# Six more groups of the first layer by seven products, one mixed weight array in place of raw weights, and first products copied from bank to bank, in a new order

## The chip, the cores and the metric

The kernel runs on one core of a Trainium2 chip. The metric is the device time of one execution in microseconds (us). Engines are called as in the profile: PE is TensorE (PEld its weight loads), DVE VectorE, ACT ScalarE, POOL GpSimd, SP SyncE, which issues most stores and the transposing transfers.

## The reference

Attention over four batches with eight heads, 768 positions and head dimension 64, each position seeing 96 local positions and 8 global ones, with a bias by distance; its output, with the heads side by side, is a matrix x of 3072 tokens by 512, which goes through a feed-forward layer with a squared relu.

```python
    scores = scale * np.matmul(q, k.transpose(0, 1, 3, 2))
    ...
    is_global = pos[None, :] < int(n_global)
    is_local = (rel >= 0) & (rel < int(n_local))
    ...
    scores = scores + bias[None, :, :, :]
    scores = np.where(keep, scores, -1000000000.0)
    ...
    return np.matmul(a, v).astype(np.float32)
...
    h = np.maximum(x @ w_in, 0.0)
    return (h * h @ w_out).astype(np.float32)
```

Here w_in is 512 by 2048 and w_out 2048 by 512.

## The kernel before

**Tiles and stages.** The 3072 tokens are worked on in eight halves of 384 (half 0 to half 7, two to a batch). For each half the scores of the local and global positions are made (PE sp, L715), put through exp on ScalarE (ex), weighed with a mask on VectorE (phat), multiplied with v (PE av, L776), divided (rec, tm), and transposed by a DMA from SP's queue into xt, the transposed x. q, k and v come in by DMAs from POOL's queue (sq, sk, v) and are transposed by SP (q<-sq, k<-sk). kb and vb hold the parts of k and v that a half needs of its neighbour.

**Layer 1.** The hidden 2048 are 16 blocks of 128. *Plain* (function layer1, L822): a block and 384 tokens are four matmuls 384 columns wide into a bank hps of PSUM; a relu (L847 on ACT, L849 on DVE) brings it to hr in SBUF, and a square of two blocks (L861, L863) to h2 (named h in the profile). *By seven products* (layer1_group): two blocks of the near half of the hidden (block 0 to 7) and the two that lie eight further (the far half) are taken as one 2 by 2 scheme with the two halves of the 512 inner and the two halves of the 384 tokens. Seven products p1 to p7 of four matmuls 192 columns wide (L925) take the place of the 16 plain ones. For them there are mixed weights (sums and differences of quarters of w_in, in_mix, made once, L886) and mixed tokens (x_mix, made for each half, L903). The products p1, p6, p7 and p4 add up in one bank, "a", p5 and p3 in a second, "f", p2 in a third, "c". In between, sums are copied to SBUF (kept, L353 on ACT, L355 on DVE) and added back by a custom add with relu on DVE (L983), or a plain relu takes the result (L989 on ACT, L991 on DVE); squares follow (L1005, L1007). In half 2 another way is used (SEEDS 1): the kept p1 is copied back into bank "f" and p2 adds onto it.

Halves 0 and 1, which open the program, are all plain (in part 256 and 128 columns wide). Half 2 has two such groups, halves 3 to 7 have three each, 17 in all; the rest of their blocks is plain.

**Layer 2** works on pairs of 128-token tiles by seven products as well (layer2_pair, L1145, with token sums mixed, L1110, and adds into y, L1207) or plain (layer2, L1059), and stores y to the output.

**The order.** Jobs of PE are listed as a program, and a table, ORDER, fixes the order of the work on all engines: words for PE's jobs (p, with a bank behind the point), DVE (d), ACT (a), SP (s), POOL's loads (l, with a job to wait for behind @) and g. Two tables of letters, LETTERS and LAYER1, set for each half the sequence in which the products of the groups and the plain blocks (s) are listed. Each engine runs its instructions strictly in its row.

## Time and profile before

| | |
|---|---|
| time, median of three runs | 202.02 us (201.25 to 203.07) |
| time of the profiled execution | 201.98 us |
| its span | 200.2 us |
| PE busy | 191.8 us (96%), clock 1.00 |
| DVE busy | 177.7 us (89%) |
| ACT busy | 146.3 us (73%) |
| POOL busy | 66.6 us (33%) |

In a group's row of the profile stand the line, engine, operation, what is written and read, the count, then busy time and the mean ns of one, then the idle time of the engine just ahead of them with what ended it. The chain of waits is read in order of time: start, length, what. Matmuls are pipelined, so that the duration of one holds part of the next; the distance between two starts is what one adds. L numbers in the profile are those of the kernel before; in the new one the same lines stand 6 to 43 further down (L353 is L359, L355 L361, L822 L833, L886 L901, L903 L921, L925 L943, L983 L1001, L989 L1007, L1007 L1025, L1110 L1139, L1145 L1175).

### The profile page before, as it was taken

Reading aid. Unit: us, or ns where it says so; the run is one execution under the profiler, and the core shown is the slowest. Engines: PE = TensorE matmul, PEld = TensorE weight load, DVE = VectorE, ACT = ScalarE, POOL = GpSimd, SP = SyncE. Lnnn points to the kernel's source line nnn. Section 1 sums busy time; section 2 is a strip of 40 time slices with the busy share of each in tenths; the row PEclk is TensorE's granted clock in tenths of the full one; section 3 lists DMA queues with packets and bytes.
Section 4 is the critical chain, followed back from the end, with each engine's and each line's share of the span. In section 5 each row is a group of like instructions: output and inputs, shape, how many; then the busy total and the mean of one; then the engine's idle time right before and its main releaser. Section 6 shows DMA issues by size and latency. Waiting matters only on the chain.

```text
span 200.2 us, 5881 instructions
## 1 busy us (share of the span) xinstructions
PE 191.8 (96%) x2349; PEld 160.8 (80%) x2349; DVE 177.7 (89%) x448; ACT 146.3 (73%) x310; POOL 66.6 (33%) x82
## 2 busy tenths in 40 slices
PE   7797999999999999999999998999999999999993
PEld 3575899856888687789877897889879899889992
DVE  6889778999995989999999997999999899899780
ACT  6899857998836679988888758987986866365311
POOL 5998537537102910970108700670000000000000
PEclk9999999999999999999999999999999999999999
DMA  5999999999998999999999995699734420020214
GB/s 161 177 149 181 198 181 171 207 194 155 149 224 89 143 123 243 134 149 105 272 119 93 152 140 114 146 150 155 199 75 142 105 75 2 0 108 0 108 52 157
DMA packets 106987, 27.52 MB, mean 137 GB/s; under 512 B 97104, under 2 KB 104016, under 8 KB 106960
## 3 DMA queue, kind: packets, MB, share of 16 engines
q0 software_dynamic: 74944, 13.11, 87.4%
q1 hardware_dynamic: 30816, 13.45, 32.1%
q10 hardware_dynamic: 1200, 0.59, 1.1%
q8 instruction: 18, 0.29, 0.7%
q14 instruction: 9, 0.07, 0.2%
HBM read 27.26 MB, written 6.29 MB: 168 GB/s over the span
## 4 chain that ended last, share of the span: by engine, by line
PE 76%; DMA 13%; POOL 6%; DVE 3%; issue 1%; SPq 0%; ACT 0%; POOLq 0%; DVEq 0%
PE yps L1145 29%; PE hps L822 17%; PE hps L925 17%; DMA w_in_sb<-in_moe_w_in_dram 5%; PE sp L715 4%; PE av L776 4%; PE yps L1059 4%; DMA q<-sq 3%; DMA xt<-tm 3%; DMA v<-in_v_dram 3%; POOL w_mix L491 2%; POOL v L491 2%; DVE hr L983 1%; PE trp L650 1%; POOL sk L491 1%
## 5 line engine op out<-in xcount | busy, mean ns | idle before, releaser
L822 PE MATMUL hps<-xt,w_in_sb 128*128 128x384 f16 (+2 forms) x336 | 45.3, 281 | 0.8 <-DMA w_in_sb<-in_moe_w_in_dram 0.8
L728 ACT ACTIVATE ex<-sp 128x512 f16<-128x512 f32 x66 | 35.3, 619 | 4.4 <-PE sp L715 3.6
L1145 PEld LDWEIGHTS <-h 128*128 128x128 f16 x376 | 34.1, 98 | 4.7
L822 PEld LDWEIGHTS <-w_in_sb 128*128 128x128 f16 x336 | 28.0, 98 | 8.7 <-DMA w_in_sb<-in_moe_w_in_dram 1.2
L1145 PEld LDWEIGHTS <-mixed 128*128 128x128 f16 x272 | 25.1, 98 | 3.1 <-DVE mixed L1110 0.2
L847 ACT ACTIVATE hr<-hps 128x384 f16<-128x384 f32 (+1 forms) x43 | 21.7, 548 | 7.6 <-PE hps L822 7.6
L983 DVE CUSTOM_DVE_ANT_0 hr<-hps,kept 128x384 f16<-128x384 f32 x49 | 25.8, 549 | 1.1 <-PE hps L925 0.7
L491 POOL DMA_DIRECT2D sq<-in_q_dram x19 | 17.0, 900 | 27.2 <-DMA xt<-tm 13.2
L353 ACT COPY kept<-hps 128x384 f32<-128x384 f32 x43 | 20.3, 491 | 7.9 <-PE hps L925 5.8
L353 ACT COPY y<-yps 128x256 f32<-128x256 f32 (+2 forms) x36 | 12.7, 381 | 18.0 <-PE yps L1145 16.5
L491 POOL DMA_DIRECT2D v<-in_v_dram x24 | 21.6, 918 | 12.1 <-DMA k<-sk 9.6
L491 POOL DMA_DIRECT2D sk<-in_k_dram x19 | 17.1, 902 | 25.2 <-DMA xt<-tm 9.4
L925 PEld LDWEIGHTS <-in_mix 128*128 128x128 f16 x272 | 23.0, 98 | 2.4 <-DVE x_mix L903 0.5
L925 PE MATMUL hps<-x_mix,in_mix 128*128 128x192 f16 x204 | 23.7, 247 | 0.2 <-DVE x_mix L903 0.2
L1145 PE MATMUL yps<-w_mix,h 128*128 128x256 f16 (+1 forms) x192 | 22.7, 264 | 0.0
L1145 PE MATMUL yps<-w_out_sb,h 128*128 128x256 f16 (+1 forms) x184 | 22.5, 268 | 0.0
L1145 PE MATMUL yps<-w_mix,mixed 128*128 128x256 f16 (+1 forms) x184 | 22.3, 268 | 0.0
L752 DVE TENSOR_TENSOR phat<-ex,mask 128x1024 f16<-128x1024 f16 (+1 forms) x36 | 21.0, 594 | 0.1
L1005 ACT ACTIVATE h<-hr 128x768 f16<-128x768 f16 x22 | 18.5, 848 | 1.2 <-DVE hr L983 0.7
L925 PEld LDWEIGHTS <-w_in_sb 128*128 128x128 f16 x204 | 17.4, 98 | 1.5
L861 ACT ACTIVATE h<-hr 128x768 f16<-128x768 f16 (+1 forms) x23 | 17.0, 768 | 1.7 <-DVE hr L849 0.9
L925 PE MATMUL hps<-xt,w_in_sb 128*128 128x192 f16 x136 | 15.8, 246 | 0.0
(110 smaller groups left out, 347.9 us busy)
## 6 DMA issues: line engine op xcount, KB each, us to landing
out_dram<-y SPq DMA_DIRECT2D x23, 256.0 KB, 2.6
v<-in_v_dram POOLq DMA_DIRECT2D x24, 128.0 KB, 6.4
sk<-in_k_dram POOLq DMA_DIRECT2D x19, 128.0 KB, 6.0
sq<-in_q_dram POOLq DMA_DIRECT2D x19, 128.0 KB, 5.0
w_in_sb<-in_moe_w_in_dram POOLq DMA_DIRECT2D x4, 512.0 KB, 10.2
w_out_sb<-in_moe_w_out_dram POOLq DMA_DIRECT2D x4, 512.0 KB, 10.5
y<-in_k_dram ACTq DMA_DIRECT2D x2, 256.0 KB, 4.8
y<-in_q_dram SPq DMA_DIRECT2D x2, 256.0 KB, 4.2
```

The source lines that it names most:

```text
L353: nc.scalar.copy(out=out, in_=in_)
L491: dma = nc.gpsimd.dma_start(out=dst, in_=src[x.b, :, r0 + t * P:r0 + (t + 1) * P, :] .rearrange("h p d -> p h d"))
L715: nc.tensor.matmul(sp[h][:, i, :], lhsT=lhsT, rhs=x.q[rows, r % HT, a, :], start=True, stop=True)
L728: nc.scalar.activation(out=st["ex"][:, h], in_=sp[h], func=AF.Exp, scale=scale)
L752: eng(e).tensor_tensor(out=x.phat[a][:, :, t0:t0 + n], op=ALU.mult, in0=st["ex"][:, :, i0:i0 + 2 * n].rearrange("p e (t b) c -> p e t (b c ...
L822: nc.tensor.matmul(st["ps"][:, i * n:(i + 1) * n], lhsT=w_in_sb[:, kk, m * P:(m + 1) * P], rhs=x.xt[:, kk, c0:c1], start=kk == 0, stop=kk ...
L847: nc.scalar.activation(out=o, in_=i, func=AF.Relu)
L861: nc.scalar.activation(out=h2, in_=hr, func=AF.Square)
L925: nc.tensor.matmul(st[name][:, i * HC:(i + 1) * HC], lhsT=left(i, kk), rhs=right(kk), start=fresh and i == kk == 0, stop=kk == KK - 1, ski ...
L983: nc.vector._custom_dve(TENSOR_ADD_SAT, out=hidden(which)[:, :, cols], in0=sums(name), in1=st[kept], s0=LARGEST, s1=0.0)
L1005: nc.scalar.activation(out=h2, in_=hr, func=AF.Square)
L1145: nc.tensor.matmul(st[bank_name][:, 0:n], lhsT=a(m), rhs=b(m)[:, cols], start=fresh and m == 0, stop=m == HK - 1, skip_group_check=not fresh)
```

## The change

Half 2 works three groups by seven products where it worked two, and halves 3 to 7 four where they worked three: 23 groups for 17. The fourth group is made of blocks 0, 1, 8 and 9 (GROUPS gets a 0), so the mixed weights are wider: 8 blocks instead of 6, 2048 elements a partition each instead of 1536. To save room, the third mixed weight is written over a quarter of the raw w_in, in two pieces, once the plain matmuls of the far half that read it are done (far_jobs); the others are three arrays in place of four.

In halves 3 to 7 (SEEDS 2, "copied"; 20 groups) p1's sum isn't kept in SBUF for p2's add; it is copied from bank "a" to a new bank "c" (across), p2 adds onto it there, and its result goes through a plain relu. p6, which reuses bank "a", also waits for that copy. For layer 2 the same form is written down but not used. Groups of matmuls in one bank now set the start flag with the bank's first matmul alone.

The table ORDER is new from end to end.

```diff
-SEEDS = [0, 0, 1, 0, 0, 0, 0, 0]
+SEEDS = [0, 0, 1, 2, 2, 2, 2, 2]
...
-GROUPS = [1, 2, 3]
-LETTERS = {3: "abcdefg", 2: "ABCDEFG", 1: "1234567"}
-LAYER1 = {2: "sasbcsdABCsesDEsFGfsgs", 3: "as123456b7cdsAeBCfgDsEFsG",
-          4: "AasBbCscDEdefF123ss45gG67", 5: "1A2BCDs3E45sF6abcdefgGs7s",
-          6: "AsabcdBeCDfsEss1F234567Gg", 7: "AsaBbcdCDseEfF1234s567Gsg"}
+GROUPS = [0, 1, 2, 3]
+LETTERS = {0: "HIJKLMN", 3: "abcdefg", 2: "ABCDEFG", 1: "1234567"}
+LAYER1 = {h: "abAcBdCeDfEgFG12H3I4J5K6L7MN" if h in [3, 5, 7, 6, 4] else "abAcBdCeDfEgFG12s3s4s5s67" for h in range(2, 8)}
...
-ORDER = """d1 s8 g2 a4 p0.0 a6 s10 d12 a0 d13 l1 d3 l4 l2 l3 d146 a26 d15 d20 a22 l0 a30 d9 d21 a18 d5 a17
...
+ORDER = """d146 g2 d1 d12 d13 d3 l1 s8 l4 a4 a6 a0 a17 d5 d22 d15 p0.0 d7 a26 a9 l3 a16 a20 l2 l5 l10 l6 l0
...
+    def copied(self, job, costs, emit, needs=()):
+
+        op = self.after(job, costs, emit, needs)
+        op.takes, op.users = 1, [[op]]
+        return op
...
+        if ms[-1] >= NFT // 2:
+            far_jobs.append((ms, job))
...
-                    mix = const.tile([P, 4, KK, near.stop - near.start], FP16, name="in_mix")
-                    in_mix.extend(mix[:, i] for i in range(4))
+                    mix = const.tile([P, 3, KK, near.stop - near.start], FP16, name="in_mix")
+                    in_mix.extend([mix[:, 0], mix[:, 1], w[1][0], mix[:, 2]])
...
+            wide = near.stop - near.start
+            for cols in [slice(0, wide)] if i != 2 else [slice(2 * P, wide), slice(0, 2 * P)]:
+                in_mix_ops[i].append(plan.add(
+                    {"DVE": 0.1 + KK * (cols.stop - cols.start) * 0.00053},
+                    lambda e, f=weight_sum, cols=cols: f(e, cols=cols),
+                    needs + w_in_op + (in_mix_ops[0] if i == 2 else []), plan.rank + MIX[4]))
...
-        seeded = SEEDS[x.hb]
+        seeded, copied = SEEDS[x.hb] == 1, SEEDS[x.hb] == 2
...
         def p1():
-            keep(run("a", True, weight(0, 0), plain(0, 0)), "a", "keep1")
+            job = run("a", True, weight(0, 0), plain(0, 0))
+            if not copied:
+                keep(job, "a", "keep1")
+                return
+
+            def across(e):
+                st["c"] = bank([P, 512], FP32, "hps")
+                copy(e, sums("c"), sums("a"))
+            ops["keep1"] = plan.copied(job, {"ACT": 0.41, "DVE": 0.48}, across)
+            st["users", "c"] = ops["keep1"].users
 
         def p2():
-            if seeded:
+            if copied:
+                give(run("c", False, weight(1, 0), plain(1, 0), [ops["keep1"]]), "c", 0, 0)
+            elif seeded:
                 give(run("f", False, weight(1, 0), plain(1, 0), [ops["seed"]]), "f", 0, 0)
             else:
                 give(run("c", True, weight(1, 0), plain(1, 0)), "c", 0, 0, "keep1")
...
+    for own, op in zip((slice(NFT // 2 + 2, NFT), slice(NFT // 2, NFT // 2 + 2)), in_mix_ops[2]):
+        op.needs.extend(job for ms, job in far_jobs
+                        if any(own.start <= m < own.stop for m in ms))
```

The new table moves rows on every engine. Two places show how; numbers behind names tell tiles apart.

ScalarE where half 3's first layer begins, beside half 2's second layer (y) and later scores (ex): before, the first product of a group (hps_1884) is kept in SBUF.

```order
L728 ACTIVATE ex_1879<-sp_1856 128x512
L728 ACTIVATE ex_1879<-sp_1857 128x512
L728 ACTIVATE ex_1899<-sp_1843 128x512
L353 COPY y_1824<-yps_1755 128x256
L353 COPY kept_1903<-hps_1884 128x384
L728 ACTIVATE ex_1815<-sp_1792 128x512
L728 ACTIVATE ex_1899<-sp_1844 128x512
L353 COPY kept_1939<-hps_1884 128x384
```

And after, where the first product (hps_1873) goes to a second bank (hps_1888):

```order
L359 COPY y_1869<-yps_1851 128x256
L735 ACTIVATE ex_1871<-sp_1790 128x512
L359 COPY hps_1888<-hps_1873 128x384
L359 COPY kept_1890<-hps_1861 128x384
L359 COPY y_1824<-yps_1813 128x256
L735 ACTIVATE ex_1871<-sp_1791 128x512
L1007 ACTIVATE hr_1921<-hps_1888 128x2x192
L359 COPY kept_1936<-hps_1873 128x384
```

The copy across stands where a keep stood, and the relu of p2 (hr_1921 from hps_1888) has come to ScalarE.

VectorE at the end of half 2's first layer, before: hr are relus or adds with relu, h2_1436 the squares that layer 2 reads, mixed_1804 the first of its token sums.

```order
L1007 TENSOR_TENSOR h2_1436<-hr_1677 128x768
L991 TENSOR_SCALAR hr_1691<-hps_1574 128x2x192
L1007 TENSOR_TENSOR h2_1436<-hr_1683 128x768
L355 COPY kb_885<-k_884 128x4x96
L355 COPY kb_885<-k_884 128x4x32
L863 TENSOR_TENSOR h2_1436<-hr_1732 128x768
L863 TENSOR_TENSOR h2_1436<-hr_1753 128x768
L1110 TENSOR_TENSOR mixed_1804<-h2_1436 128x1024
```

After, the same place:

```order
L1001 ISA hr_1763<-hps_1684,kept_1720 128x2x192
L1009 TENSOR_SCALAR hr_1741<-hps_1675 128x2x192
L1025 TENSOR_TENSOR h2_1469<-hr_1704 128x768
L1025 TENSOR_TENSOR h2_1469<-hr_1741 128x768
L1025 TENSOR_TENSOR h2_1469<-hr_1711 128x768
L878 TENSOR_TENSOR h2_1469<-hr_1722 128x768
L921 TENSOR_TENSOR x_mix_1831<-xt_1550 128x384
L1139 TENSOR_TENSOR mixed_1833<-h2_1469 128x1024
```

The four squares of the half's end stand in one row behind the relu hr_1741, with a part of the next half's x_mix between them and the token sum.

More of the change, by code (lines that the diff above doesn't have):

```diff
@@ L1126, in layer2_pair @@
         y_bufs = Buffer("y", 4), Buffer("y", 4)
[L1127 removed]
+        seeded = PAIR_SEEDS[len(seeds)] == 1 and not final
+        copied = PAIR_SEEDS[len(seeds)] == 2 and not final
         seeds.append(seeded)
@@ L1238, in p1, with across @@
             x.h2_buf.used_by(job)
-            keep(job, "a", "keep1")
+            if not copied:
+                keep(job, "a", "keep1")
+                return
+            def across(e):
+                st["c"] = bank([P, 512], FP32, "yps")
+                copy(e, st["c"][:, 0:HN], st["a"][:, 0:HN])
+            ops["keep1"] = plan.copied(job, {"ACT": 0.31, "DVE": 0.36}, across)
+            st["users", "c"] = ops["keep1"].users
         def p2():
-            if seeded:
+            if copied:
+                job = run("c", False, plain(x, i, 1), weight(1, 0), [ops["keep1"]])
+            elif seeded:
                 job = run("f", False, plain(x, i, 1), weight(1, 0), [ops["seed"]])
```

164 lines of the change are left out of this document (84 added, 80 removed).

## The prediction

> **What bounds the kernel now.** I read the page first, then the stretches of the span, the waits of TensorE and the chain that ended last. All times are of the profiled execution; 201.98 us of its time are 200.2 us of span and 1.78 us around it, and it lies 0.04 us under the median of 202.02 of the runs, so a change of the span is taken as the same change of the time.
>
> The page, its first lines of busy time and its chain of work by engine:
>
> ```profile
> span 200.2 us, 5881 instructions
> PE 191.8 (96%) x2349; PEld 160.8 (80%) x2349; DVE 177.7 (89%) x448; ACT 146.3 (73%) x310; POOL 66.6 (33%) x82
> PE 76%; DMA 13%; POOL 6%; DVE 3%; issue 1%; SPq 0%; ACT 0%; POOLq 0%; DVEq 0%
> ```
>
> TensorE is busy 96% of the span and is three quarters of the chain. The view by stretches (columns: stretch and its length, then busy us of PE, weight loads, DVE, ACT, POOL, granted clock, DMA share, GB/s) says where the other 4% lie:
>
> ```profile
> 23.60:196.80 173.20, 172.28 (x2054) 146.66 (x2054) 158.29 (x387) 126.23 (x266) 47.75 (x55) 1.00 1.16 133
> 100.00:110.00 10.00, 9.84 (x120) 7.68 (x115) 9.83 (x25) 8.73 (x21) 4.29 (x5) 1.00 1.13 108
> 110.00:120.00 10.00, 9.85 (x139) 9.21 (x137) 9.79 (x26) 6.56 (x15) 3.63 (x5) 1.00 1.92 146
> 120.00:130.00 10.00, 9.43 (x117) 7.84 (x115) 8.62 (x22) 8.98 (x19) 3.21 (x4) 1.00 0.69 130
> ```
>
> From 23.6 us to the last matmul TensorE lacks 0.92 us of 173.20, and 0.88 of these lie between 100 and 130 us. The clock is 1.00 throughout. VectorE has 158.29 of 173.20: 14.9 us of air, the next engine to run out. What comes ahead of 23.6 us is a load, in the chain (start, length, what):
>
> ```profile
> 14.16 9.41 DMA w_in_sb<-in_moe_w_in_dram
> 23.62 1.92 PE hps L822 x16
> ```
>
> So the span is: an opening set by a queue of loads, 173 us of nearly gapless matmuls, and a tail. The tail, by the timeline's last rows:
>
> ```profile
> 196.82 0.37 ACT L353 COPY y<-yps 128x256 f32<-128x256 f32 x1 [1.05 <-PE yps L1145]
> 197.22 0.33 SPq L1230 DMA_DIRECT2D out_dram<-y  x1
> ```
>
> The last matmul ends at 196.8, a copy, a store, and the span's end at 200.2: 3.4 us.
>
> **The change, part by part.** *Fewer, narrower products.* A group by seven products has 28 matmuls of 192 columns in place of 16 of 384. Six groups more make 96 of the wide ones go and 168 narrow ones come; by the order of the programs 384-wide ones fall from 144 to 48 and 192-wide ones rise from 476 to 644, and all other shapes keep their counts but for two warming matmuls of the opening. Since a pipelined matmul's own duration overlaps the next, the price is the distance from start to start, in TensorE's timeline:
>
> ```profile
> 127.07 1.49 PE L925 MATMUL hps<-xt,w_in_sb 128*128 128x192 f16 x16
> 128.39 1.46 PE L822 MATMUL hps<-xt,w_in_sb 128*128 128x384 f16 x8
> 129.69 0.49 PE L925 MATMUL hps<-x_mix,in_mix 128*128 128x192 f16 x4
> ```
>
> Sixteen narrow ones take 1.32 us (82.5 ns each), eight wide ones 1.30 (162.5 ns). 96 x 162.5 = 15.60 us go, 168 x 82.5 = 13.86 come: **-1.74 us**, all of it on the path, since nearly all of layer 1 lies behind 23.6 us.
>
> Each new matmul also brings a weight load, which could set the pace of narrow ones:
>
> ```profile
> L925 PEld LDWEIGHTS <-in_mix 128*128 128x128 f16 x272 | 23.0, 98 | 2.4 <-DVE x_mix L903 0.5
> ```
>
> A load lasts 98 ns, more than 82.5, and still sixteen pairs in a row went by in 1.32 us, so loads overlap one another or the matmul by enough here. The Trainium skill ("TensorE: Matmul & The Clock Gate", section "LDWEIGHTS (loading the stationary operand)") gives a load as its columns over 1.2, which would be an estimated 107 ns for 128 columns; were that the pace, 168 x 107 = 18.0 us would come for 15.6 that go, and the first term would be +2.4 us; the trace does not agree that the loads set the pace.
>
> *Waits between 100 and 130 us.* Their rows, and the transfers that the chain names ahead of them:
>
> ```profile
> 107.24 0.81 PE L822 MATMUL hps<-xt,w_in_sb 128*128 128x384 f16 x4
> 108.22 0.51 PE L925 MATMUL hps<-x_mix,in_mix 128*128 128x192 f16 x4 [0.16 <-DVE x_mix L903]
> 111.28 0.19 PE L776 MATMUL av<-vb,phat 128*128 128x65 f16 x1
> 111.62 0.19 PE L776 MATMUL av<-v,phat 128*128 128x65 f16 x1
> 120.73 1.04 PE L1145 MATMUL yps<-w_out_sb,h 128*128 128x256 f16 x8
> 122.34 0.57 PE L715 MATMUL sp<-q,k 64*128 64x128 f16 x14 [0.57 <-DMA q<-sq]
> 100.06 5.36 DMA xt<-tm
> 106.57 5.01 DMA v<-in_v_dram
> 116.73 5.47 DMA q<-sq
> ```
>
> Four wide matmuls are 0.65, so 0.33 us is lost at 108.22; 0.31 at 111.62; and at 122.34, after eight 256-wide ones (0.89, below), 0.72, of which 0.08 is an entry into scores (below): 1.28 in all. In the new order the loads of half 6 no longer stand behind the transposes of xt on their queue, and summing the matmuls between by the distances above, 14.2 and 11.3 us of TensorE work lie between the attention products of the two late transposes and the first matmuls that read them, where 12.8 and 10.0 lie now. That is more than what is lost at each, so I take **-1.0** of the 1.28; the ends are -1.28, and +0.3 if another load turns late.
>
> *Entries into scores.* Eight 256-wide matmuls before other work and before scores:
>
> ```profile
> 82.01 1.05 PE L1145 MATMUL yps<-w_out_sb,h 128*128 128x256 f16 x8
> 82.90 1.04 PE L1145 MATMUL yps<-w_mix,mixed 128*128 128x256 f16 x8
> 83.87 0.34 PE L715 MATMUL sp<-q,k 64*128 64x128 f16 x6
> ```
>
> 0.89 us against 0.97: 0.08 us for entering a run of score matmuls. The new order cuts the scores into 24 runs where there are 20: **+0.3**.
>
> *Sums copied from bank to bank.* In halves 3 to 7 (20 groups) the first product's sum is copied to a second bank, 17 times by ScalarE and three times by VectorE, and the second product adds onto it; its result then needs a plain relu where it needed VectorE's add with relu. The copy across banks does not occur before; its nearest rows, by line (busy us, mean ns, idle before):
>
> ```profile
> L353 ACT COPY kept<-hps 128x384 f32<-128x384 f32 x43 | 20.3, 491 | 7.9 <-PE hps L925 5.8 <-DVE hr L983 1.6
> L353 ACT COPY hps<-kept 128x384 f32<-128x384 f32 x2 | 1.0, 482 | 0.5 <-DVE hr L983 0.5
> L355 DVE COPY kept<-hps 128x384 f32<-128x384 f32 x8 | 4.4, 552 | 0.9 <-PE hps L925 0.9
> L983 DVE CUSTOM_DVE_ANT_0 hr<-hps,kept 128x384 f16<-128x384 f32 x49 | 25.8, 549 | 1.1 <-PE hps L925 0.7 <-ACT h L1005 0.2
> L989 ACT ACTIVATE hr<-hps 128x384 f16<-128x384 f32 x13 | 6.4, 489 | 2.1 <-PE hps L925 2.1
> ```
>
> A copy out of a bank takes 491 ns and one into a bank 482, so I take 482 for one that does both (552 on VectorE). It adds a wait: p2, which waited only for a free bank, now waits for it, and behind p2 all TensorE work. A product of four shows 0.49 us and its successor starts after 0.33, so its last sum is there 0.16 after that; with 0.03 to start (196.79 to 196.82 in the tail), 0.48 of copy and some 0.06 to release TensorE the turnaround is 0.74 us. By the new order the TensorE work between p1's end and the first matmul that needs the copy (p2, or p6, which reuses p1's bank) is 0.87 us at the least (twice), 0.95 and 0.98 next, and 1.5 at the middle of the twenty. So the work laid between hides it, by 0.13 at the worst, if the copy starts at once: **+0.1**. Uncovered, all twenty would cost 20 x 0.74 = 15 us; below nothing there is no end, since today p2 doesn't wait for it at all.
>
> *VectorE's and ScalarE's load.* Beside the rows above:
>
> ```profile
> L1005 ACT ACTIVATE h<-hr 128x768 f16<-128x768 f16 x22 | 18.5, 848 | 1.2 <-DVE hr L983 0.7 <-DVE hr L991 0.4
> L1007 DVE TENSOR_TENSOR h<-hr 128x768 f16<-128x768 f16 x12 | 6.5, 552 | 0.2
> L847 ACT ACTIVATE hr<-hps 128x384 f16<-128x384 f32 x29 | 13.4, 508 | 5.3 <-PE hps L822 5.3
> L355 DVE CAST sq<-y 128x512 f16<-128x512 f32 x2 | 1.1, 562 | 0.7 <-DMA y<-in_q_dram 0.7
> L355 DVE COPY xt<-trx 128x256 f16<-128x256 f16 x3 | 0.8, 281 | 0.0
> L886 DVE TENSOR_TENSOR in_mix<-w_in_sb 128x1536 f16<-128x1536 f16 x2 | 1.9, 955 | 0.6 <-DMA w_in_sb<-in_moe_w_in_dram 0.6
> 80.68 1.02 DVE L863 TENSOR_TENSOR h<-hr 128x768 f16<-128x768 f16 x2
> ```
>
> By the order VectorE gets 8 more 768-wide squares (8 x 0.55), 3 copies across and 3 more keeps (6 x 0.55), and loses 3 adds with relu, 7 plain relus (10 x 0.55) and two casts of sq (0.56 each): +2.2 - 1.1. The mixed weights are three arrays of 2048 elements (955 x 2048/1536 = 1.27 each) and one made in place in two pieces of 1536 and 512 (0.96 and some 0.4) in place of four of 0.955: +1.4. Four copies of xt come over from ScalarE, +1.1; a few copies of heads more and one of y less about cancel. In all +3.6 us, so the 14.9 us of air become about 9 in a stretch shorter by 2. ScalarE has 29 more narrow relus and 17 copies (+22.4), and 19 wide relus, 8 squares and 5 keeps less (-18.9): +3.5 of 47 us of air. Over the whole span that is cover enough, and I take **+0.2** for VectorE's lost air. The in-place pieces wait for the plain matmuls that read the raw weights; both of them and what is queued behind them on VectorE wait in the order for matmuls that come later still, so they cost nothing of their own.
>
> *The end of half 2's first layer.* The one place where the order itself is short (about 80 us). VectorE has to do, behind the last product's relu, four squares in a row, and TensorE reads the fourth with its second run of eight 256-wide matmuls. In between TensorE has 24 scores (0.75 with 0.030 each), four narrow matmuls (0.33), eight 256-wide ones (0.89) and two entries (0.16): 2.1 us. VectorE needs 0.16 until the sum is there, 0.47 for the relu and each of three squares (two in a row last 1.02, so 0.47 apart) and 0.55 for the last: 2.6 us. **+0.5**, by a shortfall of 2.6 - 2.1; the ends are 0, if a relu ran ahead, and 0.9 with the x_mix and the token sum behind it. In the order before two of the squares stand further ahead.
>
> *Opening and tail.* The third chunk's successor moves behind three small loads on POOL's queue, but the same eleven token loads, v and one chunk stand before the chunk that the chain waits for: 0. Two chunks of w_out move behind v; the last lands just as it is needed: 0 to +0.3. The tail ends on VectorE's add of 128x256 in place of a copy by ScalarE, 0.05 us more.
>
> Sum: -1.74 - 1.0 + 0.3 + 0.1 + 0.2 + 0.5 + 0.05 = -1.6 us; a span of 198.6 and a time of **200.3 us**.
>
> **The rivals.** *More than forecast.* All of the 1.28 goes, and the 0.5 at half 2's end and the 0.2 do not come, since VectorE was ahead: -1.74 - 1.28 + 0.3 = -2.7, time 199.3. For it: TensorE waited nowhere for VectorE but 0.2 us at 108.22. Against: the order is short there by its own sums.
>
> *Given back at the ends of the halves.* The shortfall of half 2's end comes at the ends of the other five group halves too, at 0.5 each: +2.5, time 202.8. For it: VectorE's air falls by a third. Against: at those ends the order keeps the squares apart.
>
> *Late copies: slower.* Copies stand in ScalarE's strict order between exponentials and squares. With a square ahead (0.85 us) the turnaround is 0.74 + 0.85 = 1.59. Eleven of the twenty gaps are shorter (0.87, 0.87, 0.95, 0.98, 1.16, 1.20, 1.22, 1.27, 1.31, 1.53, 1.53); what they lack comes to 4.6 us, which takes the place of the 0.1: time 204.8. It decides from a turnaround of 1.5 us on, where the lack is 3.7. A copy also needs its second bank free, and for the first gap of 0.87 an add with relu of VectorE, late in its own queue, frees it. For it: the keeps already waited 1.6 us for VectorE's adds, in their row above; and right ahead of that same copy stand two copies of kb, which waited for a transpose in one case of three:
>
> ```profile
> L353 ACT COPY kb<-k 128x384 f16<-128x384 f16 x3 | 1.5, 510 | 1.7 <-DMA k<-sk 1.7
> ```
>
> Against: 27% of ScalarE's span is idle, and ahead of the other copy with 0.87 stand plain relus whose products are done.
>
> *Weight loads set the pace.* At 98 ns for each of the 168: 16.5 come for 15.6 that go, +0.9 in place of -1.74, time 202.9. Against it: the sixteen in 1.32 us.
>
> **How the numbers follow.** Forecast 0.50 (its own range 199.3 to 201.4: the unknown costs' lower ends together, and half of their upper ends, which hardly all come at once), more 0.20, given back 0.17, late copies 0.10, weight loads 0.03. One per cent, about what a measurement tells from no change, is 2.0 us: below 200.0 is faster, above 204.0 slower. Faster: the 0.20 and two fifths of the forecast's 0.50, 0.40; slower: the late copies and a little of the two before, 0.12; the rest, 0.48, is within. The range is 198.4 to 203.2: it takes in the rivals up to 202.9 and leaves out the late copies and the outer end of the second.
>
> **What would show it.** In the new profile: 192-wide matmuls still 82 to 83 ns apart, and PE's sum of busy time in the gapless stretch some 1.7 us less; no wait for q<-sq, v or x_mix above 0.1 us between 100 and 130 us; a wait of half a microsecond for h or mixed at about 80 us; copies hps<-hps of some 480 ns with TensorE waiting for them less than 0.2 us in all; VectorE near 181 us busy. The forecast is wrong if TensorE waits for hps copies, or for squares at the end of more halves, or if the opening's chunk lands later than 23.6.

## The result, and the profile after

The changed kernel took 203.62 us in the median of 20 runs (201.94 to 206.97), the kernel before 203.11 us in 20 (201.25 to 205.78): a ratio of 1.0066 with a 95% interval of 1.0041 to 1.0092. It is slower by some 1.3 us, less than one per cent, where 1.7 us less was forecast. Ratios here are formed from undisturbed runs alone, medians from all of them, so a ratio need not be the quotient of two medians.

The profiled execution of the changed kernel is the fastest of its 20 runs, 201.94 us, and its span is that of before. The page's first lines of busy time and its chain by engine, and from the groups by line, shapes kept apart, the copies from bank to bank:

```profile
span 200.2 us, 6057 instructions
PE 192.6 (96%) x2419; PEld 166.5 (83%) x2419; DVE 180.7 (90%) x458; ACT 148.7 (74%) x320; POOL 66.8 (33%) x82
PE 76%; DVE 14%; DMA 3%; ACT 3%; issue 2%; ACTq 0%; DVEq 0%
```

```profile
L359 ACT COPY hps<-hps 128x384 f32<-128x384 f32 x17 | 8.1, 477 | 1.9 <-PE hps L943 1.6
L361 DVE COPY hps<-hps 128x384 f32<-128x384 f32 x3 | 1.7, 557 | 0.0
```

In the chain, DMA had 13% before and DVE 3%; now DVE has 14%. The chain's early pieces show where (start, length, what): VectorE's copies, reciprocals and products of the opening, one behind the other up to 28 us, in place of a load of w_in.

```profile
17.09 0.42 DVE tm L1515
...
20.75 1.00 DVE ph L1480 x3
...
27.73 0.61 DVE hr L864
28.38 1.03 PE hps L833 x8
```

By stretches, the three tens that held before's late waits:

```profile
100.00:110.00 10.00, 10.00 (x132) 8.52 (x130) 9.83 (x24) 9.95 (x24) 7.32 (x9) 1.00 2.07 152
110.00:120.00 10.00, 9.80 (x143) 9.47 (x141) 9.86 (x27) 7.38 (x18) 1.75 (x2) 1.00 1.32 176
120.00:130.00 10.00, 10.00 (x139) 8.99 (x137) 9.83 (x26) 9.17 (x21) 3.59 (x5) 1.00 1.50 120
```

TensorE lacks 0.20 us of these thirty where it lacked 0.88. So far that part of the forecast came; what the experiments say of it stands at the end.

Busy time hides half of the story, since pipelined matmuls overlap. The table below is worked out from the starts of all of TensorE's matmuls in the trace. Each shape has its distance from start to start in an unbroken row (82 ns for 192 columns, 163 for 384, 109 for 256, 56 for 128, 216 for 512, 30 for scores and for products with v). "Work" is the sum of these distances over the program; the columns behind it are the microseconds in each stretch that these distances do not cover, so idle time and the extra time at changes between kinds of matmul (into and out of scores, for one). The distances are rounded, so a column holds to about 0.1 us. "Last" is the start of the last matmul. The work of e9 holds its 1.63 us without use.

```
                                  work   last  0-40  40-80  80-100  100-130  130-end
before                           183.4  196.5   8.7    1.2     0.7      2.1      0.5
before, profiled again (e2)      183.4  196.5   8.4    1.2     0.6      2.2      0.7
after                            181.4  196.4  10.4    1.2     1.2      1.4      0.9
after, profiled again (e1)       181.4  198.9  10.9    1.2     3.4      1.2      1.0
after, old first 9 us (e5)       183.5  197.5   8.6    1.2     2.0      1.2      1.0
after, vb later (e6)             181.4  198.4  10.0    1.2     3.9      1.0      1.0
after, e5's and e6's edits (e7)  183.5  198.7   8.9    1.2     2.6      1.4      1.1
before, new opening (e4)         183.3  197.2  10.9    1.0     0.4      1.1      0.6
after, old opening (e3)          181.5  198.6   9.4    1.9     3.0      1.8      1.0
after, old opening mended (e8)   181.5  197.4   9.2    1.9     2.9      1.0      1.0
after, useless work (e9)         183.0  198.0  10.2    1.5     0.8      1.4      1.1
after, loads early (e10)         181.4  197.0   9.8    1.8     1.2      1.9      0.9
both (e11)                       181.5  196.0   9.4    1.2     1.1      1.9      1.0
both, two entries moved (e12)    181.5  195.6   9.0    1.6     1.1      1.6      0.7
```

The change does save TensorE 2.0 us of work: by the table's distances 96 x 163 - 168 x 82 ns = 1.87 us through the narrower products (1.74 with the prediction's 162.5 and 82.5), and 0.11 through two warming matmuls fewer. And it saves 0.7 us between 100 and 130. It loses 1.7 us (first profiles) to 2.5 us (second ones) ahead of 40 us, and 0.5 us in one execution and 2.8 in another between 80 and 100. Of the loss at 80 to 100 us, 0.5 us in both executions are half 2's squares, which the prediction had; the other 2.3 and the opening are what the experiments are about.

### The profile page after: what moved, and what is told of

Read it like the earlier page. It is cut to its first block, busy times and chain, and to the rows that moved or that the text cites. A ratio compares the mean times of both kernels' runs of the same rounds, so it can differ in the third digit from the quotient of the medians.

```text
span 200.2 us, 6057 instructions
## 1 busy us (share of the span) xinstructions
PE 192.6 (96%) x2419; PEld 166.5 (83%) x2419; DVE 180.7 (90%) x458; ACT 148.7 (74%) x320; POOL 66.8 (33%) x82
## 4 chain that ended last, share of the span: by engine, by line
PE 76%; DVE 14%; DMA 3%; ACT 3%; issue 2%; ACTq 0%; DVEq 0%
PE yps L1175 30%; PE hps L943 23%; PE hps L833 9%; PE av L783 4%; PE yps L1088 4%; PE sp L721 3%; DMA y<-in_k_dram 3%; DVE phat L759 2%; DVE tm L1515 2%; DVE ph L1480 2%; PE sp L1430 2%; ACT hr L1007 1%; DVE vb L361 1%; DVE h L1025 1%; DVE hr L864 1%
## 5 line engine op out<-in xcount | busy, mean ns | idle before, releaser
L1175 PEld LDWEIGHTS <-h 128*128 128x128 f16 x376 | 33.4, 98 | 4.5 <-DVE h L878 0.4
L943 PEld LDWEIGHTS <-w_in_sb 128*128 128x128 f16 x368 | 31.0, 98 | 1.7 <-issue 0.6
L833 PE MATMUL hps<-xt,w_in_sb 128*128 128x256 f16 (+2 forms) x240 | 26.9, 262 | 0.1
L1001 DVE CUSTOM_DVE_ANT_0 hr<-hps,kept 128x384 f16<-128x384 f32 x46 | 24.3, 550 | 1.5 <-PE hps L943 1.4
L1007 ACT ACTIVATE hr<-hps 128x384 f16<-128x384 f32 x42 | 19.7, 495 | 6.1 <-PE hps L943 6.0
L833 PEld LDWEIGHTS <-w_in_sb 128*128 128x128 f16 x240 | 18.8, 98 | 3.9 <-issue 0.2
L943 PE MATMUL hps<-xt,w_in_sb 128*128 128x192 f16 x184 | 21.9, 246 | 0.0
L943 PE MATMUL hps<-x_mix,w_in_sb 128*128 128x192 f16 x184 | 21.4, 246 | 0.3 <-DVE hr L1001 0.2
L943 PE MATMUL hps<-x_mix,in_mix 128*128 128x192 f16 x184 | 21.4, 246 | 0.0
L359 ACT COPY kept<-hps 128x384 f32<-128x384 f32 x38 | 17.6, 483 | 4.9 <-PE hps L943 4.6
L1023 ACT ACTIVATE h<-hr 128x768 f16<-128x768 f16 x25 | 20.8, 849 | 0.3 <-DVE hr L1001 0.2
```

The costliest lines, as they stand in the source:

```text
L359: nc.scalar.copy(out=out, in_=in_)
L833: nc.tensor.matmul(st["ps"][:, i * n:(i + 1) * n], lhsT=w_in_sb[:, kk, m * P:(m + 1) * P], rhs=x.xt[:, kk, c0:c1], start=kk == 0 and i == ...
L943: nc.tensor.matmul(st[name][:, i * HC:(i + 1) * HC], lhsT=left(i, kk), rhs=right(kk), start=fresh and i == kk == 0, stop=kk == KK - 1, ski ...
L1001: nc.vector._custom_dve(TENSOR_ADD_SAT, out=hidden(which)[:, :, cols], in0=sums(name), in1=st[kept], s0=LARGEST, s1=0.0)
L1007: nc.scalar.activation(out=o, in_=i, func=AF.Relu)
L1023: nc.scalar.activation(out=h2, in_=hr, func=AF.Square)
```

## The experiments

The theories were three. The new opening makes TensorE late (the prediction had put it at 0). The transfers of half 4, which TensorE reads from 80 us on, come too late for a TensorE that has less to do; the first profile shows nothing of it, but it is that of a quick execution. And a lower clock in the opening, which the new profile shows, does it.

### The same kernel again, and the kernel before again

Neither is edited.

> The changed kernel once more. Theory O (the opening took the gain back): a time about 0.3 to 0.7% over the kernel before, 203 to 204 us beside 202.5 to 203; in its profile the granted clock again under 0.9 between 5 and 15 us, TensorE's layer 1 late there, and behind 30 us no more lost than in the profile that is known. Theory B (the body took it back, in most executions): a slower execution than the one profiled, with waits of TensorE for VectorE or ScalarE of more than 1 us in all behind 40 us.

> The kernel before against itself: ratio 1.000 within 0.3%, which says how much of 0.66% can be chance. Both theories: clock 1.00 between 5 and 15 us, the layer's first matmuls set by the landing of the second chunk of w_in at 23.5 us.

The changed kernel: 203.71 us, ratio 1.0055 (1.0004 to 1.0106), profiled span 202.7. The kernel before as its own control: 1.0001 (0.9964 to 1.0037), profiled span 200.2. With the control at 1, the difference is not one of chance between runs. Both theories of the first expectation came in part: the time lies in the range given for the opening, but behind 40 us there are new waits. The second profiled execution of the changed kernel took 204.58 us, 0.9 above the median, where the first lay 1.7 below it. TensorE's waits behind 40 us there (engine, line, waited for: us, times, longest); the first profile had in this list only 0.2 us for an hr:

```profile
PE hps L943 <- DVE x_mix L921: 0.9, 1, 0.9
PE hps L943 <- DMA xt<-tm: 0.5, 1, 0.5
PE hps L943 <- ACT hps L359: 0.2, 1, 0.2
```

All three lie between 80 and 91 us. The last is a copy of half 2, which still keeps p1 in SBUF and copies it back into a bank, so not one of the new copies from bank to bank:

```profile
82.28 0.47 ACT L359 COPY hps<-kept 128x384 f32<-128x384 f32 x1
```

VectorE's timeline at that place, then TensorE's (start, length, engine, line; in brackets the idle time before and what ended it):

```profile
80.29 0.28 DVE L361 COPY vb<-v 32x520 f16<-32x520 f16 x1 [1.72 <-DMA v<-in_v_dram]
```

```profile
81.82 0.82 PE L943 MATMUL hps<-x_mix,w_in_sb 128*128 128x192 f16 x8 [0.94 <-DVE x_mix L921]
82.81 0.49 PE L943 MATMUL hps<-xt,w_in_sb 128*128 128x192 f16 x4 [0.17 <-ACT hps L359]
90.19 0.41 PE L943 MATMUL hps<-xt,w_in_sb 128*128 128x192 f16 x3 [0.46 <-DMA xt<-tm]
```

x_mix is only the last link. VectorE runs its row strictly, and stood 1.72 us at a copy vb of a part of v whose load had not landed; the adds with relu and x_mix that TensorE wanted were queued behind it. In the first profile the same copy did not wait.

One part of why the load is late shows on GpSimd's queue. Half 4's first load of q waits until half 3's q has been transposed out of the one buffer that both use. Its rows in before, in the first profile of after, and in the second:

```profile
60.86 0.87 POOL L491 DMA_DIRECT2D sq<-in_q_dram  x1 [10.11 <-DMA q<-sq]
```

```profile
61.89 0.88 POOL L497 DMA_DIRECT2D sq<-in_q_dram  x1 [11.41 <-DMA q<-sq]
```

```profile
64.22 0.88 POOL L497 DMA_DIRECT2D sq<-in_q_dram  x1 [13.88 <-DMA q<-sq]
```

The other loads of q, k and v follow on that queue, then on SP's queue the transposes of k and q and of xt. The last of the chain, three transposes of xt issued together, is issued as follows in the same three:

```profile
79.37 11.35 SPq L801 DMA_TRANSPOSE xt<-tm  x3
```

```profile
80.69 9.13 SPq L810 DMA_TRANSPOSE xt<-tm  x3
```

```profile
82.71 9.83 SPq L810 DMA_TRANSPOSE xt<-tm  x3
```

So the end of the chain moved 1.3 us later in the first execution and 3.3 in the second, while TensorE's work ahead of it had become less.

The later start is not all of it. Of half 4's six loads of q and k the last starts at 67.99 us in before and lands at 72.41, after 4.4 us. In the first profile of after it even starts earlier, at 66.35, but takes 7.0 us and lands at 73.38; in the second it starts at 68.61, takes 7.3 and lands at 75.94. In all three profiles of the old body (before, e2, e4) these six loads take 4.2 to 4.4 us in the mean, in all eleven of the new body 5.7 to 6.9. The old order lets them pause for a transpose of xt, as the first row below shows, and brings the third v only at 80.29 us; the new one issues six loads of q and k and three of v in one row. The page's median for all loads of q, before and after, moves the same way:

```profile
64.53 0.88 POOL L491 DMA_DIRECT2D sk<-in_k_dram  x1 [2.79 <-DMA xt<-tm]
```

```profile
sq<-in_q_dram POOLq DMA_DIRECT2D x19, 128.0 KB, 5.0
```

```profile
sq<-in_q_dram POOLq DMA_DIRECT2D x19, 128.0 KB, 7.0
```

That nine loads in a closed row slow each other would fit this, but no run changes the row alone.

### New opening on the old body, and old opening on the new body

The table's first words, some 180, are those that set the opening to about 30 us. The kernel before was given those of the changed kernel, and the changed kernel those of before (banks named in another permutation so that the two parts fit).

```diff
-ORDER = """d1 s8 g2 a4 p0.0 a6 s10 d12 a0 d13 l1 d3 l4 l2 l3 d146 a26 d15 d20 a22 l0 a30 d9 d21 a18 ...
+ORDER = """d146 g2 d1 d12 d13 d3 l1 s8 l4 a4 a6 a0 a17 d5 d22 d15 p0.7 d7 a26 a9 l3 a16 a20 l2 l5 ...
```

```diff
-ORDER = """d146 g2 d1 d12 d13 d3 l1 s8 l4 a4 a6 a0 a17 d5 d22 d15 p0.0 d7 a26 a9 l3 a16 a20 l2 l5 ...
+ORDER = """d1 s8 g2 a4 p0.1 a6 s10 d12 a0 d13 l1 d3 l4 l2 l3 d146 a26 d15 d20 a22 l0 a30 d9 d21 a18 ...
```

> The kernel before with the order of the opening of the changed kernel (same cut). Theory O: 1.2 to 1.6 us slower than the kernel before, ratio 1.006 to 1.008. Theory B: the same as the kernel before, ratio 0.998 to 1.002, as the opening waits for w_in in any case.

> The changed kernel with the order of the opening (the first 179 words of the table, to about 32 us, on all engines) of the kernel before; the groups, copies and everything behind are as changed. Theory O: the 1.5 us that the opening took are back, 0.7 to 0.8% faster than the changed kernel and 0.1 to 0.4% faster than the kernel before; clock 1.00 between 5 and 15 us and the second chunk of w_in at 23.5 us in the chain again. Theory B: no faster than the changed kernel, 0.5% slower than the kernel before.

The old body with the new opening: 1.0088 (1.0047 to 1.0129), about 1.8 us slower with no other change. In the table it loses 2.2 to 2.5 us more ahead of 40 us. Its timeline of TensorE, and ahead of it that of before, at the places where the first scores of the program are made:

```profile
6.06 1.05 PE L1390 MATMUL sp<-early,slope_id 128*128 128x128 f16 x16
8.85 0.40 PE L1411 MATMUL sp<-q,k 64*128 64x128 f16 x8 [0.56 <-DVE k L355]
```

```profile
7.08 0.40 PE L1325 MATMUL trp<-ident,sq 128*128 128x128 f16 x4 [0.88 <-ACT sq L353]
8.36 1.05 PE L1390 MATMUL sp<-early,slope_id 128*128 128x128 f16 x16 [0.41 <-DVE early L424]
10.17 0.40 PE L1411 MATMUL sp<-q,k 64*128 64x128 f16 x8 [0.76 <-ACT k L353]
```

In the changed kernel's own timelines of ScalarE and VectorE the casts that are waited for:

```profile
5.66 0.92 ACT L440 ACTIVATE mask<-dmask 128x384 f16<-128x384 f32 x2
6.49 0.60 ACT L359 CAST sq<-y 128x512 f16<-128x512 f32 x1
```

```profile
6.93 0.57 DVE L361 CAST sk<-y 128x512 f16<-128x512 f32 x1 [0.54 <-DMA y<-in_k_dram]
7.52 0.79 DVE L430 CAST early<-dmask 128x384 f16<-128x384 f32 x1
```

Both casts of sq have gone from VectorE to ScalarE, the second behind masks, and the distances (early) are cast on VectorE behind the second cast of sk. The first scores of q and k come 1.3 us later for it, at 10.17 in place of 8.85; in the changed kernel at 10.18. None of these waits is for w_in: its second chunk lands at 23.2 to 23.3 us with the new opening, not later than the 23.57 of before, and TensorE comes late to it. Up to 40 us TensorE waits for w_in once, at 31.75:

```profile
PE hps L822 <- DMA w_in_sb<-in_moe_w_in_dram: 0.2, 1, 0.2
```

That is the fourth chunk. The new order issues it at 20.1 us, not 16.5, and it lands at 31.7, not 29.3; the chain of this execution runs through it. So behind the late casts stands a second limit, nearly as late: in this execution TensorE could not have started that product earlier, whatever the casts did. The profiled execution is also the quickest of its twelve (202.66 us, median 204.59): its last matmul starts only 0.7 us after before's, as 1.0 us come back between 100 and 130 us, so it does not show where the whole 1.8 us of a usual run lie.

The new body with the old opening: 1.0035 (0.9996 to 1.0074), outside the 0.996 to 0.999 of the theory, and not told apart from the changed kernel or from the kernel before. The joint costs 0.8 us near 27 us (two products share a bank there), and at 80 to 100 us it loses 3.0. In this profile, then, what a better opening gains is waited away.

### The old opening, mended at the seam

```diff
- ... a88 a108 p59.3 p50.1 d105 p49.4 d106 ...
+ ... a88 a108 p50.1 d105 p49.4 p59.3 d106 ...
```

> The changed kernel with the order of the opening (to about 32 us) of the kernel before, as in the third experiment, with one PE job moved so that the seam of the two orders no longer holds TensorE up for 0.95 us at 26.5 us. Theory D (what TensorE gains ahead of 80 us is waited away at 80 to 92 us for half 4's transfers: loads, transposes of q and k, and the xt behind them on the same queue): at 40 us TensorE is 2 us ahead of the kernel before, and between 80 and 92 us it waits 2.5 to 4 us; time within 0.5 us of the third experiment, ratio 1.000 to 1.004. Rival (the opening is all of the loss): 0.95 us faster than the third experiment, ratio 0.996 to 0.999.

1.0042 (1.0007 to 1.0078). TensorE's waits of over half a microsecond behind 40 us:

```profile
PE hps L943 <- DMA xt<-tm: 1.0, 1, 1.0
PE hps L943 <- DVE x_mix L921: 0.7, 2, 0.6
```

The seam is gone, the waits for half 4's transfers stay, 1.7 us of them (VectorE stood 1.36 us at the copy vb ahead of that x_mix). That is less than the 2.5 to 4 us expected; the time is, as the theory had it, within 0.2 us of the third experiment, with a ratio at the upper end of its 1.000 to 1.004, and the rival's 0.996 to 0.999 is excluded.

### The old words for the first 9 us only

> The changed kernel with only the first 62 words of the table (to about 9 us: which engine casts sq, when the slopes, the distance mask and the first distance products come, and the loads of that time) in the order of the kernel before. Theory O1 (the loss of the opening begins there: TensorE has done 1.2 us less by 10 us, and from then on it is TensorE and VectorE that are late and not w_in): 1.2 to 1.7 us faster than the changed kernel, ratio to the kernel before 0.998 to 1.001. Rival O2 (the loss comes from the order between 9 and 32 us, VectorE's above all): as the changed kernel, ratio 1.004 to 1.008.

The first 62 words are those of before, the rest the new table's. 1.0055 (1.0021 to 1.0089), as the changed kernel: the rival's range, not the theory's. The program fills a gap that it foresees with warming transposes, and put 44 in where the changed kernel has 7, 37 x 56 ns = 2.1 us of work. They cost nothing here, since TensorE still waits behind them for a load of k, which lands at 17.25 us. Their row, and that wait:

```profile
L379 PE MATMUL trp<-ident,early 128*128 128x128 f16 x44 | 3.1, 232 | 0.0
```

```profile
PE trp L1408 <- DMA w_mix<-in_k_dram: 0.5, 1, 0.5
```

Counted as in the table, warming left out, TensorE has done 3.0 us of work by 10 us in before, 1.8 in the changed kernel and 2.8 here; by 20 us it is 9.4, 8.6 and 8.4. So the 1.2 us that the new first 9 us cost are nearly all had back by 10 us, and are gone again by 20 us. Whether the order behind 9 us would take it in any case, or only because the two orders don't fit here, stays open: which entries of the opening cost the time is not shown.

### The copy of v out of VectorE's way, and both

One word moves the copy vb, at which VectorE stood, 54 entries further down; a second kernel does that together with the old first 9 us.

```diff
- ... l53@221 l49 d328 d292 l50 ... l57@278 d334 ...
+ ... l53@221 l49 d292 l50 ... l57@278 d328 d334 ...
```

> The changed kernel with one word of the table moved: VectorE's copy vb<-v for half 3 (two instructions) comes behind the first two token sums of half 2, some 6 us later, and still ahead of the attention product that reads it. Theory V (VectorE stands still in its row for a v that lands late, 1.7 us in the second profile of the changed kernel, and the x_mix behind it keeps TensorE waiting 0.9 us and more): no wait of TensorE for x_mix at about 81 us in the profile, 0.5 to 1.2 us faster than the changed kernel in the median, ratio 1.000 to 1.004. Rival (the copy takes its 0.5 us from VectorE at the end of half 2, where it is short anyway, or the late transfer delays others as much): ratio 1.005 or more.

> Both edits: first 62 words as before and the copy of vb later. If both theories hold the gains add up: 1.7 to 2.9 us faster than the changed kernel, ratio 0.992 to 0.998, which is what the forecast had for the change without these two losses. If O1 fails and V holds: as the edit of vb alone.

1.0059 (1.0022 to 1.0095) and 1.0060 (1.0022 to 1.0099): no gain. The wait for x_mix is gone, and in its place stand (the first of the two kernels, behind 40 us):

```profile
PE hps L943 <- DMA xt<-tm: 1.3, 1, 1.3
PE sp L721 <- DMA q<-sq: 1.2, 1, 1.2
```

So it was not that one copy. v, q and xt are all late, and in these profiles another is waited for where the first no longer is.

### Useless work ahead of half 4's first scores

Ten more matmuls of 384 columns, 10 x 163 ns = 1.63 us, go into a bank that the scores then overwrite.

```diff
+            if x.hb == 4 and not delayed:
+                delayed.append(1)
+                for _ in range(10):
+                    nc.tensor.matmul(sp[0].rearrange("p i c -> p (i c)")[:, 0:HALF],
+                                     lhsT=w_in_sb[:, 0, 0:P], rhs=w_in_sb[:, 1, 0:HALF],
+                                     start=True, stop=True)
```

> The changed kernel with ten more matmuls of 384 columns (1.63 us of work without use) ahead of half 4's first scores at about 81 us. Theory D: most of them lie in a wait that comes anyway: 0 to 0.8 us over the changed kernel in the median. Rival (TensorE's own work or VectorE set the time there): 1.6 us over the changed kernel, ratio to the kernel before 1.013 to 1.015.

1.0108 (1.0065 to 1.0151), over six runs. Against the changed kernel's 1.0055 that is about 1.1 us for 1.63, between the theory's and the rival's, but the intervals overlap, and the time alone does not say how much of it was hidden. The profile lists no wait of TensorE from 20 us on, and in the table it loses 0.8 us at 80 to 100, where the changed kernel lost 1.2 and 3.4. That fits late transfers, for which TensorE would have waited otherwise, but it is one execution.

### Half 4's loads of k earlier

Half 4's three loads of k go ahead of those of q on GpSimd's queue, and wait for half 3's transpose of k alone, which frees their buffer; the loads of q wait for that of q, as before.

```diff
- ... p93.7 l44@227 a145 l40@230 l43@218 l41@230 l45@217 l42@227 p102.4 ...
+ ... p93.7 l40@230 a145 l41@230 l42@227 l43@218 l44@227 l45@217 p102.4 ...
-                    for turn in halves[x.hb - 1].turns + (prev.xturns if AFTER[x.hb] else []):
+                    for turn in halves[x.hb - 1].turns[:1 if x.hb == 4 else 2] + (prev.xturns if AFTER[x.hb] else []):
```

> The changed kernel, where half 4's three loads of k come ahead of those of q on POOL's queue and wait for the transpose of half 3's k alone (some 2 us earlier than that of q). Theory D: k<-sk of half 4 is issued 1.5 to 2.5 us earlier (71 to 72 us instead of 73.5 to 76), and what waits on it shrinks: 0.8 to 1.7 us faster than the changed kernel, ratio 0.998 to 1.002. Rival (the waits at 80 to 92 us come from VectorE's row): as the changed kernel.

> Both: the old opening (mended) and half 4's loads of k first. If the opening took 1.7 us and the transfers the rest, this is what the change was forecast to be: 2 to 3 us faster than the changed kernel, ratio 0.990 to 0.996. If only one of the two holds: 0.997 to 1.003.

With the new opening: 1.0033 (1.0003 to 1.0064), an interval that excludes neither the theory's range nor the changed kernel's 1.0055; the transpose of k, expected at 71 to 72 us, is issued at 73.25, behind one of xt in SP's row. With the mended old opening as well: 0.9999 (0.9965 to 1.0032), a profiled span of 199.7. The old opening alone gave 1.0042 on the same chip. In the kernel with both no wait for a transfer is left behind 40 us; its list, and the loads and the transposes of xt:

```profile
PE hps L943 <- DVE kept L361: 0.3, 1, 0.3
PE hps L943 <- DVE x_mix L921: 0.2, 1, 0.2
```

```profile
59.45 2.67 POOL L497 DMA_DIRECT2D sk<-in_k_dram  x3 [9.12 <-DMA k<-sk]
62.67 2.67 POOL L497 DMA_DIRECT2D sq<-in_q_dram  x3 [0.55 <-DMA q<-sq]
78.86 10.05 SPq L810 DMA_TRANSPOSE xt<-tm  x3
```

The loads start at 59.45 and the three transposes are issued at 78.86, ahead of before's 60.86 and 79.37. Each of the two repairs alone leaves the kernel slower than before; the two together bring it back to before's time. Worked out from the same runs, all on one chip (means, with 95% intervals), the early loads gain 1.1 us (0.4 to 1.7) where the opening is the old one, and the old opening gains 0.8 (0.2 to 1.5) where the loads are early. So both are causes. That the second hides the first, so that one repair alone gains nothing, is not shown: the single gains over the changed kernel, 0.1 to 0.3%, are too near the noise to tell this from gains that add up. And the expectation for both, 0.990 to 0.996, missed: 0.9999 lies in the range meant for the case that only one theory holds. The loss is repaired; the gain that the change was forecast to have is not there. In the table this kernel has 1.9 us less work than before, and loses 0.7 to 1.0 us more ahead of 40 us, 0.4 to 0.5 more at 80 to 100 (half 2's squares, as forecast) and 0.3 to 0.5 more behind 130.

### Two more entries moved

v's tile 2 of half 1 ahead of the fourth chunk of w_in on GpSimd's queue, and the last square of half 2 ahead of a relu on VectorE.

```diff
- ... d72 l17 p29.5 ... d58 l15 l18 ... p145 d315 ... a336 d300 d314 ...
+ ... d72 l15 p29.5 ... d58 l17 l18 ... p145 d300 d315 ... a336 d314 ...
```

> This is the kernel of the experiment before it (the changed layer 1, the old opening, half 4's loads of k ahead of the others on GpSimd's queue) with two entries more moved: the load of v's tile 2 for half 1 stands ahead of the fourth chunk of w_in on GpSimd's queue, and on VectorE the last square of half 2's layer 1 stands ahead of a relu that is wanted later. Theory (what is left at these two places are waits, 0.7 us for v at 29.6 us and 0.45 us for the squares at 82 us): TensorE loses 0.6 us less at 29 to 30 us and 0.2 to 0.4 us less at 82 us, so that the time is 0.6 to 1.0 us under that kernel's, 0.993 to 0.997 of the kernel before's. Rival (each queue gives the wait to its next entry): the fourth chunk of w_in or another transfer is waited for instead, and the ratio stays at 0.998 to 1.002.

201.61 us, 0.9966 (0.9928 to 1.0004), profiled span 199.3. The middle lies in the theory's range, the interval reaches into the rival's, so the time does not tell them apart; and it is not shown to be faster than the kernel before, though it is the fastest of all that ran. The profile speaks for the rival: the wait for v is gone, and behind it stand 0.4 us for an xt of VectorE; the squares that TensorE reads at 82 us are waited for 0.2 us at another of them.

```profile
30.28 1.05 PE L833 MATMUL hps<-xt,w_in_sb 128*128 128x256 f16 x8 [0.38 <-DVE xt L361]
82.43 1.70 PE L1175 MATMUL yps<-w_out_sb,h 128*128 128x256 f16 x14 [0.23 <-DVE h L1025]
```

## Why the prediction was right or wrong

*Fewer, narrower products: right.* Narrow products still go by at 82 to 83 ns, here twelve between 79.85 and 80.84, 0.99 us, and TensorE's work fell by 2.0 us, of which this step is 1.74 to 1.87, as worked out under the table. Weight loads do not set the pace. One sign that I gave for it could not show it: PE's busy time in a gapless stretch of fixed length is full either way (172.21 us of 23.6 to 196.4 for 171.90 before), where 1.7 less was forecast.

```profile
79.85 1.15 PE L943 MATMUL hps<-x_mix,w_in_sb 128*128 128x192 f16 x12
80.84 0.49 PE L943 MATMUL hps<-xt,w_in_sb 128*128 128x192 f16 x4
```

*Waits between 100 and 130 us: right on the transfers, in part by luck in its size.* Forecast -1.0 us; the table gives -0.7 in the first profile and -1.0 between the second ones. No wait for q<-sq, v or x_mix is left there. But the old body with the new opening (e4) loses 1.0 us less there as well, with nothing of the order changed behind 32 us: a TensorE that comes later finds its data there. The cleaner case is the kernel with both repairs (e11), in which TensorE comes early: no transfer is waited for there, as forecast, but a copy of VectorE is (kept, 0.3 us), and with smaller delays behind VectorE 1.9 us are lost, only 0.2 to 0.3 less than before.

*Copies from bank to bank: right.* 477 ns for the forecast 482, 557 on VectorE for 552; in no profile of any run did TensorE wait for one of them. The 0.17 us at 82.81 in the second execution was for half 2's copy out of kept. The rival of late copies is excluded.

*The end of half 2's first layer: right.* Sixteen 256-wide matmuls, 2 x 0.87 us in an unbroken row, take 2.23 from 82.58 to 84.81: 0.49 us late, for the squares, against +0.5. The waits of the weight loads name them:

```profile
PEld L1175 <- DVE h L878: 0.4, 1, 0.4
PEld L1175 <- DVE h L1025: 0.3, 1, 0.3
```

*VectorE's and ScalarE's load: about right.* VectorE is 180.7 us busy where near 181 was forecast, ScalarE 2.4 us more than before where 3.5 was. The +0.2 for lost air cannot be told apart from other small losses.

*Entries into scores: too small.* By the starts a run of scores costs 0.10 us at its entry and another 0.12 at its end, which the sum left out; behind 23.6 us there are 16 runs for 13, and all of it comes to +0.5 us against +0.3.

*Opening: wrong, and the first step that failed.* "The same eleven token loads, v and one chunk stand before the chunk that the chain waits for: 0" counted loads alone. That chunk did come when it came before; what I had not followed is VectorE's and ScalarE's order ahead of it, which makes the tokens ready for TensorE, and the chunk behind the three small loads ("the third chunk's successor"), which lands 2.5 us later. The step cost 1.7 to 2.5 us in the table, and by itself made the kernel before 1.0088 times as slow. That the new opening as a whole costs this is shown by that run; how it divides among casts, copies and loads is not. The sign I gave for being wrong ("if the opening's chunk lands later than 23.6") looked at the wrong thing.

*A term that was not there: half 4's transfers, the second step that failed.* I searched the trace of before for waits that exist, between 100 and 130 us, and asked which of them go. At 80 to 100 us there was none, since transfers came just in time. The chain from half 3's transpose of q over nine loads and two transposes to xt had little to spare; in the new order its loads take 5.7 to 6.9 us in place of 4.2 to 4.4, in most executions they also start later, and TensorE comes there with less work behind it. The same move of loads ahead of the transposes of xt that I booked as a gain for half 6 was made for half 4. Against before, the table has 0.5 us more lost in the first profile and 2.8 in the second. Half 2's squares are 0.5 of each, so these transfers cost nothing in the first and 2.3 us in the second. The other kernels with the new body and the loads as they were lose 2.0 to 3.9 in that stretch in all (e3, e5, e6, e7, e8), so the first profile is the exception. The rival "given back at the ends of the halves" (202.8) came nearest in time, by a mechanism that is not there: no further half's squares stand among TensorE's waits. (The forecast's own sum, -1.6 on 202.0, gives 200.4 and not 200.3.)

By the table's rows the second profiles come out as: -2.0 of work, +2.5 ahead of 40 us, +2.8 at 80 to 100, -1.0 at 100 to 130, +0.3 behind, in all +2.6, where their last matmuls lie 2.4 us apart (the rest is rounding); the first ones as -2.0, +1.7, +0.5, -0.7, +0.4, in all -0.1, as their last matmuls. The 1.3 us of the ratio lie between the two.

## What to carry to other kernels

When TensorE's work shrinks, the waits to look for are those that do not exist yet: follow for every stage the chain from the freed buffer over load and transpose to the first reader, and compare its slack with what TensorE gains. An opening can be set by the engines that prepare its data as much as by its loads, so when an order is rewritten, each cast and copy ahead of the first matmul has to be followed. When a row of loads is moved up, the time of one load has to be looked at again and not only its place. And the profile of one quick execution can lack a wait that slower ones have; a second profile of the same kernel shows it.

## What was not expected of the hardware

The same program's transfers differ between executions by more than the change is worth. Half 4's first load started at 61.89 us in one execution of the changed kernel and at 64.22 in another, with the span at 200.2 and 202.7 us; before was at 60.86 in the one that is quoted. Between the two of the changed kernel, 2.0 of the 2.3 us are the transpose of half 3's q ahead of it, issued at 57.15 and at 57.52 us, which took 4.1 us to land in one and 6.0 in the other.

The new opening was seen with a lower clock in one of its kernels and not in another, and lost the same time in both. Stretches of the changed kernel and of the old body with the new opening (last columns: clock, DMA share, GB/s):

```profile
0.00:10.00 10.00, 7.13 (x47) 4.17 (x47) 6.76 (x21) 6.07 (x14) 7.93 (x15) 0.92 1.39 168
```

```profile
0.00:10.00 10.00, 6.34 (x47) 3.36 (x47) 6.91 (x21) 6.08 (x14) 7.93 (x15) 1.00 1.41 169
```

A clock of 0.92 makes the 47 matmuls longer, 7.13 us of busy time for 6.34, but as many are done by 10 us in both: TensorE waits there for casts and copies, and the lower clock fills waiting time. Ahead of 40 us the table shows 10.4 and 10.9 us lost at the lower clock and 10.9 at full clock, so the theory of the clock falls with it.
